# A one-core attention and gated-convolution kernel gets a new written order: first loads, zero fills and all later steps

## The chip, the cores and the metric

The kernel runs on one core of one Trainium2 chip. TensorE multiplies matrices, VectorE and ScalarE work on tiles, GpSimd takes a few two-operand rows and issues some transfers, and SyncE (SP) issues most transfers. The metric is device microseconds of one execution. Shown for the kernel before is the median of three runs; a profile is of one further execution.

## The reference

Inputs are `q`, `k`, `v` of 4 batches x 8 heads x 768 positions x 64, eight memory keys and values for each head, two 512x512 weights and a filter of 5 taps for each of 512 channels. Weights and filter come as 64-bit floats. Cut to what is computed:

```python
for c in range(S // 32):                      # chunks of 32 queries
    k_ctx = k[:, :, max(0, 32*c - 16) : min(S, 32*c + 40)]
    k_full = concatenate([mem_k, k_ctx]); v_full = ...same for v...
    scores = 0.125 * q_c @ k_full.T
    a = softmax(scores)
    out[chunk] = a @ v_full
x = out as (B, S, 512)
gate = sigmoid(sum over 5 taps of conv_w[t] * x shifted by t)     # causal
result = (gate * (x @ w_val)) @ w_out
```

## The kernel before

**Units.** Attention is cut into 20 units: one pair of heads and a span of positions (the first 256 positions of the first batch for units 0 to 3, its other 512 for units 4 to 7, and all 768 of one batch for units 8 to 19). For each unit `u` TensorE transposes K and Q (`tk`, `tq`) into PSUM, the steps `ek` and `eq` evict them, `sc` multiplies the scores, `mx` and `ss` on VectorE take maximum and shift, `ex` on ScalarE the exponential, `tp` transposes the probabilities, `ep` evicts them, `va` multiplies with V, `nd`, `ni`, `nx` divide by the sum, and `tx` transposes the result `x`. From `x` come a rounded part `xh`, its remainder `xl`, and the filter's sum in `gate`: the first tap `cv<u>_0_4` writes it, four more add to it on VectorE (L817, the last is `cv<u>_0`); `ga` is a tanh on ScalarE. `hs` and `hp` carry four columns over a span's edge.

**Pieces.** The two products with the weights run over eight pieces of positions (256, 512 and six of 384). `f1_n_co,ci` (L867) is three products of piece `n`: high with high, high with low, low with high. `h` multiplies by the gate, `hh` and `hl` split the result again, `f2` (L922) multiplies by the second weight, `oe` evicts, `st` stores.

**Weights.** Each of the eight 128-row blocks (`wv0` to `wv3`, `wo0` to `wo3`) is loaded raw (`lw0` to `lw7`, two buffers), and decoded in steps 1 to 8 on VectorE and ScalarE (step 1, L346, takes the exponent out, step 2, L352, the mantissa, step 7, L373, sets the sign, step 8, L379, is a product on VectorE or GpSimd); `h` and the bare name split it into a rounded part (a cast) and a remainder (L255). The filter goes the same way (`cw1` to `cw8`), is transposed by TensorE and copied.

**V tiles.** Three tiles in turn hold V in windows. Before the first three units they are filled with zeros and a column of ones (`zv0` to `zv2`, L276); loads `lv` put the windows in, and from unit 3 on `mv` copies the memory values in first. `mk` copies the memory keys, which TensorE has transposed once (`tmem`, evicted by `emem`), into the K tiles.

**What sets the order.** The string `ORDER` (lines 71 to 171) is the program's order, written out: each word names an engine (T TensorE, V VectorE, A ScalarE, G GpSimd, S SP) and a step, and each engine takes its own steps in that order. `Plan.run` issues them; waits between engines follow from the data and the buffers in `CAPS` (one buffer each for `x`, for the scores and values, for the transposes; three PSUM banks for the products). An engine that waits holds up everything behind it in its own queue, its transfers too.

## Time and profile before

| | us |
|---|---|
| median of three runs (268.54 to 270.05) | 268.61 |
| the profiled execution: its own time | 270.8 |
| its span, first to last instruction | 268.8 |
| TensorE busy (share of the span) | 240.4 (89%) |
| TensorE weight loads | 202.8 (75%) |
| VectorE | 209.9 (78%) |
| ScalarE | 130.4 (49%) |
| GpSimd | 74.2 (28%) |
| moved by transfers | 34.97 MB, 130 GB/s on the mean |

The profiled execution is 2.2 us longer than the median. Matmuls overlap in their pipeline, so TensorE's busy time hides short waits; the busy time of its weight loads shows better how densely it is fed. A row of a timeline or chain begins with its start in us from the first instruction and its length in us; an arrow `<-` in brackets names what ended the idle time before it. A row of a group gives count, total busy us and mean ns. A name ending in q (SPq, ACTq) is that engine's queue issuing a transfer.

### The profile page before, as it was taken

How to read it: one execution, taken by the hardware profiler on the slowest of the kernel's cores; microseconds unless marked ns; L12 is line 12 of the kernel's file. 1: busy time of each engine (PE TensorE's matmuls, PEld its weight loads, DVE VectorE, ACT ScalarE, POOL GpSimd, SP SyncE). 2: the span in 40 equal slices, each digit the busy share in tenths (PEclk: the TensorE clock that was granted, in tenths of full speed). 3: DMA queues.
4: the chain of work that ended last, by engine and by line, in shares of the span. 5: the costliest groups of instructions: out<-in, count | busy, mean ns of one | idle time of the engine just before them, and what ended most of it. 6: DMA issues, size and time to landing. Idle time of an engine off the chain costs nothing.

```text
span 268.8 us, 10223 instructions
## 1 busy us (share of the span) xinstructions
PE 240.4 (89%) x4478; PEld 202.8 (75%) x4478; DVE 209.9 (78%) x376; ACT 130.4 (49%) x240; POOL 74.2 (28%) x98
## 2 busy tenths in 40 slices
...
GB/s 155 173 167 196 202 181 197 184 208 158 140 197 178 156 151 156 195 109 206 114 160 124 58 147 160 184 182 179 25 82 80 2 2 80 79 0 41 39 78 78
DMA packets 88657, 34.97 MB, mean 130 GB/s; under 512 B 83794, under 2 KB 85350, under 8 KB 88614
## 3 DMA queue, kind: packets, MB, share of 16 engines
...
q10 hardware_dynamic: 320, 0.33, 0.5%
q14 instruction: 8, 0.07, 0.1%
HBM read 28.03 MB, written 6.29 MB: 128 GB/s over the span
## 4 chain that ended last, share of the span: by engine, by line
PE 51%; DVE 23%; DMA 8%; ACT 7%; issue 7%; SPq 1%; POOL 1%; POOLq 0%; ACTq 0%; DVEq 0%
PE vp L867 18%; PE op L922 12%; DVE gate L817 9%; PE sp L658 5%; PE xps L709 4%; PE tpx L769 4%; DMA v<-in_v_dram 4%; PE tp L588 3%; DMA mk_nat<-in_mem_k_dram 3%; DVE xl L255 2%; DMA kn<-in_k_dram 2%; PE tk L588 2%; PE tk L582 2%; ACT gate L821 2%; DVE xn L732 2%
## 5 line engine op out<-in xcount | busy, mean ns | idle before, releaser
L817 DVE SCALAR_TENSOR_TENSOR gate<-tpx,cw,gate 128x764 f32<-128x764 f32 (+4 forms) x80 | 67.7, 846 | 4.6 <-ACT gate L821 3.9
L867 PE MATMUL vp<-xh,wv_hi 128*128 128x384 f32 (+2 forms) x128 | 48.1, 376 | 0.1
L867 PE MATMUL vp<-xl,wv_hi 128*128 128x384 f32 (+2 forms) x128 | 44.1, 345 | 1.5 <-DVE xl L255 1.5
L867 PE MATMUL vp<-xh,wv_lo 128*128 128x384 f32 (+2 forms) x128 | 43.5, 340 | 0.0
L922 PE MATMUL op<-wo_hi,hh 128*128 128x512 f32 (+1 forms) x100 | 41.4, 414 | 0.0
L255 POOL TENSOR_TENSOR hl<-h,hh 128x384 fp32r<-128x384 f32 (+2 forms) x23 | 23.3, 1017 | 63.8 <-ACT hh L237 48.1
L922 PE MATMUL op<-wo_hi,hl 128*128 128x512 f32 (+1 forms) x100 | 38.5, 385 | 0.0
L922 PE MATMUL op<-wo_lo,hh 128*128 128x512 f32 (+1 forms) x100 | 38.5, 385 | 0.0
L963 POOL DMA_DIRECT2D out_dram<-o x22 | 12.1, 550 | 68.6 <-ACT o L952 43.7
L867 PEld LDWEIGHTS vp<-xl,wv_hi 128*128 128x128 f32 x128 | 24.3, 190 | 3.6 <-DVE xl L255 2.8
L867 PEld LDWEIGHTS vp<-xh,wv_hi 128*128 128x128 f32 x128 | 24.4, 190 | 2.3 <-ACT xh L237 0.3
L867 PEld LDWEIGHTS vp<-xh,wv_lo 128*128 128x128 f32 x128 | 24.5, 191 | 1.1 <-issue 0.2
L873 DVE SCALAR_TENSOR_TENSOR h<-gate,vp 128x384 f32<-128x384 f32 (+2 forms) x32 | 17.4, 547 | 9.5 <-PE vp L867 9.3
L237 ACT CAST hh<-h 128x384 fp32r<-128x384 f32 (+2 forms) x25 | 12.6, 508 | 21.7 <-DVE h L873 21.4
L658 PEld LDWEIGHTS sp<-kT,qT 64*32 64x32 f32 x1536 | 16.5, 107 | 8.0 <-issue 3.1
L658 PE MATMUL sp<-kT,qT 64*32 64x64 f32 x1536 | 20.0, 228 | 2.6 <-issue 0.9
L841 ACT ACTIVATE gate<-gate 128x768 f32<-128x768 f32 (+2 forms) x20 | 14.3, 716 | 16.5 <-DVE gate L817 13.5
L237 ACT COPY pT<-tp 128x384 f32<-128x384 f32 (+2 forms) x29 | 13.9, 478 | 16.5 <-PE tp L588 16.5
L922 PEld LDWEIGHTS op<-wo_hi,hl 128*128 128x128 f32 x100 | 18.8, 188 | 4.0
L709 PE MATMUL xps<-v,pT 64*32 64x65 f32 x1536 | 20.2, 229 | 0.9 <-DMA v<-in_v_dram 0.4
L709 PEld LDWEIGHTS xps<-v,pT 64*32 64x32 f32 x1536 | 16.8, 107 | 5.1 <-issue 2.2
L922 PEld LDWEIGHTS op<-wo_hi,hh 128*128 128x128 f32 x100 | 18.8, 188 | 2.3
(101 smaller groups left out, 436.3 us busy)
## 6 DMA issues: line engine op xcount, KB each, us to landing
out_dram<-o POOLq DMA_DIRECT2D x20, 256.0 KB, 3.0
...
```

The source lines that it names most:

```text
L237: return lambda: nc.scalar.copy(out(), in_())
L255: return lambda: eng.tensor_tensor(out=out(), in0=a(), in1=b(), op=ALU.subtract)
L588: nc.tensor.transpose(U[name, i][:, (g - g0) * P : (g - g0 + 1) * P], src(g), ident)
L658: nc.tensor.matmul(U["sp"][CH * jc : CH * (jc + 1), j, g * WIN : (g + 1) * WIN], U["qT"][j * D : (j + 1) * D, g * P + CH * jc : g * P + CH ...
L709: nc.tensor.matmul(U["xps"][CH * jc : CH * (jc + 1), j, g * VW : (g + 1) * VW], U["pT"][j * D : (j + 1) * D, g * P + CH * jc : g * P + CH ...
L769: nc.tensor.transpose(U["x", i][:, o : o + P], U["xn"][:, g].rearrange("p j d -> p (j d)"), ident,)
L817: nc.vector.scalar_tensor_tensor(out=o, in0=i_, scalar=w, in1=o, op0=ALU.mult, op1=ALU.add)
L841: nc.scalar.activation(g, g, AF.Tanh, scale=0.5)
L867: nc.tensor.matmul(vp, w, x, start=ci == 0 and m == 0, stop=ci == NCT - 1 and m == 2)
L873: nc.vector.scalar_tensor_tensor(out=T["h", n, co][:, 0:nt], in0=bt[b, co]["gate"][:, t0 : t0 + nt], scalar=1.0, in1=T["vp", n, co][:, 0:n ...
L922: nc.tensor.matmul(op, x, w[:, ci, c0:c1], start=ci == 0 and m == 0, stop=ci == NCT - 1 and m == 2)
L963: eng.dma_start(out[b, r0 : r0 + P, c0:c1], T["o", n, g, c0][:, 0 : c1 - c0])
```

## The change

Two edits. The zero fill of the V tiles shrinks: the whole tile is no longer filled; tile 0 gets zeros in its first window alone, and all three get their column of ones. And `ORDER` is another string, in nearly every line. Its 1141 steps are the same, but their places differ, and 96 of them run on another engine.

```diff
 ORDER = """
-V:bias0 G:ident S:lcw A:bias S:lk0 A:lq0 G:zv0 V:zv1 S:lq1 A:lk1 G:zk V:zm S:mem S:lv1_1 G:lw0
-V:cw1 A:cw4 V:cw2 G:lw1 V:cw3 S:lmv G:zv2 T:tk0_0 V:cw6 A:cw5 V:cw7 S:lv0_1 V:cw8 A:ek0_0 S:lv2_1
...
-G:st7_2 T:f2_7_02 T:f2_7_21_ T:f2_7_03 T:f2_7_22_ A:oe7_0 T:f2_7_23_ G:st7_0 A:oe7_2_ G:st7_2_
+V:bias0 G:ident G:lw0 S:mem S:lcw S:lk0 A:lq0 G:zv0 S:lv0_0 S:lv0_1 A:lk1 S:lq1 S:lw1 V:zv1
+S:lv1_0 S:lv1_1 V:zv2 S:lv2_0 S:lv2_1 V:zm A:bias G:zk V:cw1 G:lmv A:cw4 V:cw2 V:cw3 V:cw6 T:tk0_0
+A:cw5 V:cw7 G:cw8 A:ek0_0 S:lk2 T:tcw A:cw T:tk1_0 V:wv01 A:wv04 V:wv02 V:wv03 A:ek1_0 V:wv06
...
+A:oe7_0 T:f2_7_10 S:st7_0 T:f2_7_21_ T:f2_7_11 T:f2_7_22_ T:f2_7_12 T:f2_7_23_ T:f2_7_13 A:oe7_2_
+G:st7_2_ A:oe7_1 G:st7_1
 """
...
     for i in range(NV):
-        def zero_v(eng, t=v_tiles[i]):
-            eng.memset(t, 0.0)
+        def zero_v(eng, t=v_tiles[i], i=i):
+
+            if i == 0:
+                eng.memset(t[:, 0, 0:D], 0.0)
             eng.memset(t[:, :, D : D + 1], 1.0)
```

Three places show what the new string does on an engine. The first is VectorE from its fill of the memory values on, at the first weight; `craw`, `e_cw` and `m_cw` are the filter, `tp_mem` and `memT` the memory keys, `raw_wv0` the first weight. Before:

```order
L296 MEMSET mv_78 128x1024
L346 TENSOR_SCALAR e_cw_132<-craw_86 20x128
L352 TENSOR_SCALAR m_cw_133<-craw_86 20x128
L357 SCALAR_TENSOR_TENSOR m_cw_133<-craw_86,m_cw_133 20x128
L368 TENSOR_SCALAR e_cw_132<-e_cw_132 20x128
L373 SCALAR_TENSOR_TENSOR e_cw_132<-craw_86,e_cw_132 20x128
L379 TENSOR_TENSOR m_cw_133<-m_cw_133,e_cw_132 20x128
L240 COPY cw_77<-tp_cw_168 128x20
L240 COPY memT_75<-tp_mem_171 64x64 x2
L240 COPY kT3_71<-memT_75 128x24x8
L346 TENSOR_SCALAR e_wv0_196<-raw_wv0_130 128x512
```

The same place of VectorE now:

```order
L298 MEMSET mv_78 128x1024
L348 TENSOR_SCALAR e_cw_150<-craw_86 20x128
L354 TENSOR_SCALAR m_cw_151<-craw_86 20x128
L359 SCALAR_TENSOR_TENSOR m_cw_151<-craw_86,m_cw_151 20x128
L370 TENSOR_SCALAR e_cw_150<-e_cw_150 20x128
L375 SCALAR_TENSOR_TENSOR e_cw_150<-craw_86,e_cw_150 20x128
L348 TENSOR_SCALAR e_wv0_195<-raw_wv0_99 128x512
```

The filter's product and copy have gone to GpSimd and ScalarE, and the copies of the memory keys stand after the second weight now.

The second place is TensorE's start; `kn` and `qn` are raw K and Q, `sp0` the scores of unit 0. Before:

```order
L582 MATMUL tk0_0_144<-ident_67,kn0_101 64x64 x12
L439 MATMUL tp_cw_168<-ident_67,m_cw_133 128x20
L315 MATMUL tp_mem_171<-ident_67,mk_nat_76 128x128
L582 MATMUL tq0_0_182<-ident_67,qn0_104 64x64 x8
L658 MATMUL sp0_203<-kT0_68,qT0_199 32x64 x16
```

The same place of TensorE now:

```order
L584 MATMUL tk0_0_159<-ident_67,kn0_103 64x64 x12
L441 MATMUL tp_cw_179<-ident_67,m_cw_151 128x20
L584 MATMUL tk1_0_182<-ident_67,kn1_118 64x64 x12
L584 MATMUL tq1_0_203<-ident_67,qn1_121 64x64 x8
L584 MATMUL tq0_0_224<-ident_67,qn0_106 64x64 x8
L317 MATMUL tp_mem_250<-ident_67,mk_nat_76 128x128
L584 MATMUL tk2_0_259<-ident_67,kn2_176 64x64 x12
L660 MATMUL sp0_277<-kT0_68,qT0_247 32x64 x16
```

The first scores stand behind the transposes of units 1 and 2 as well.

The third place is VectorE at the end of piece 3; `h3_3` is that piece's last block, `ss14` the shift of unit 14's scores. Before:

```order
L679 TENSOR_REDUCE mx14_2659<-sp14_2585 128x12
L240 CAST xh20_2671<-tpx12_0_2469 128x768
L683 TENSOR_TENSOR ss14_2681<-sp14_2585,mx14_2659 128x2x6x64
L255 TENSOR_TENSOR xl20_2690<-tpx12_0_2469,xh20_2671 128x768
L240 COPY kT3_71<-tk15_1_2683 128x12x2x16
L873 SCALAR_TENSOR_TENSOR h3_2_2743<-gate12_2115,vp3_2_2562 128x384
L240 CAST hh3_2_2749<-h3_2_2743 128x384
L725 TENSOR_SCALAR den13_2755<-xps13_2693 128x12
L240 COPY pT14_2759<-tp14_0_2745 128x384
L728 RECIPROCAL den13_2755<-den13_2755 128x12
L732 TENSOR_TENSOR xn13_2766<-xps13_2693,den13_2755 128x2x6x64
L873 SCALAR_TENSOR_TENSOR h3_3_2781<-gate13_2315,vp3_3_2651 128x384
```

The same place of VectorE now:

```order
L875 SCALAR_TENSOR_TENSOR h3_1_2684<-gate11_1768,vp3_1_2636 128x384
L819 SCALAR_TENSOR_TENSOR gate20_2646<-tpx12_0_2617,cw_77,gate20_2646 128x767
L240 CAST hh3_1_2699<-h3_1_2684 128x384
L240 CAST xh20_2705<-tpx12_0_2617 128x768
L255 TENSOR_TENSOR xl20_2763<-tpx12_0_2617,xh20_2705 128x768
L677 MEMSET sp14_2714 32x2x16
L679 MEMSET sp14_2714 32x2x8
L681 TENSOR_REDUCE mx14_2771<-sp14_2714 128x12
L825 TENSOR_SCALAR gate21_2788<-tpx13_0_2774,cw_77 128x768
L255 TENSOR_TENSOR xl21_2797<-tpx13_0_2774,xh21_2786 128x768
L875 SCALAR_TENSOR_TENSOR h3_3_2806<-gate13_2310,vp3_3_2668 128x384
```

The shift of unit 14 and one eviction of its probabilities now come after this block, and the first tap and remainder of unit 13 before it.

More of the change, by code (lines that the diff above doesn't have):

```diff
@@ new lines @@
+V:wo27 A:cv1_0_4 V:ni2 S:lv5_1 V:mk8 A:ep4_0 V:nx2 V:cv1_0_0 A:wo25 T:va3 V:wo16 A:xh1_0 T:tq5_0
+S:lv5_0 V:cv1_0_1 G:wo28 A:mv6 V:nd3 V:xl1_0 V:cv1_0_2 T:f1_0_11 A:eq5_0 V:ni3 S:lq7 V:cv1_0
+T:f1_0_31 A:wo2h V:wo17 T:f1_0_01 A:ga1 S:lv6_0 T:tx2_0 G:wo2 T:tk8_0 V:wo18 A:xh2_0 A:hs2 A:ek8_0
+S:lw7 A:cv2_0_4 T:tq6_0 S:lk9 V:xl2_0 A:wo1h V:nx3 T:f1_0_32 S:lk10 V:cv2_0_0 A:eq6_0 G:wo1
+T:f1_0_12 V:cv2_0_1 T:va4 S:lq8 V:cv2_0_2 T:tq7_0 S:lv6_1 V:cv2_0 A:mv7 V:nd4 V:ni4 T:tx3_0
+T:f1_0_02 A:ga2 S:lv7_1 V:nx4 A:xh3_0 A:cv3_0_4 V:xl3_0 T:sc5 V:cv3_0_0 S:lv7_0 V:hs3 V:cv3_0_1
@@ new lines @@
+A:ga4 S:lv8_0 V:mx6 G:mk10 T:tx5_0 A:eq8_0 T:f2_0_03 V:hp5 V:ss6 A:cv5_0_4 T:tk10_0 V:xh5_0
+T:f2_0_12 A:ex6 V:oe0_0 A:ek10_0 T:va7 V:xl5_0 S:st0_0 T:tp6_0 V:cv5_0_0 G:mv10 T:f2_0_13 V:nd7
+V:ep6_0 T:f1_1_00 A:oe0_1 V:ni7 V:cv5_0_1 T:tq9_0 T:f1_1_10 V:nx7 G:st0_1 A:eq9_0 S:lv10_0
+T:f1_1_30 V:cv5_0_2 T:va6 V:cv5_0 S:lv10_1 T:tk11_0 A:ga5 V:nd6 G:mv9 T:tx7_0 V:ni6 A:ek11_0
+T:f1_1_31 A:xh7_0 V:hp7 V:nx6 T:tq9_1 A:cv7_0_4 V:xl7_0 T:f1_1_11 A:eq9_1 V:cv7_0_0 T:f1_1_01
+S:lv9_1 T:sc9 V:cv7_0_1 S:lv9_0 V:cv7_0_2 T:tk11_1 V:mx9 G:mk13 A:ek11_1 T:tq8_1 V:cv7_0 A:eq8_1
@@ new lines @@
+A:ep11_1 T:f1_2_00 T:tq13_0 T:tx10_0 A:eq13_0 T:va11 S:lv13_0 A:xh10_0 A:cv10_0_4 V:xl10_0
+T:tq12_0 S:lv13_1 G:mv14 T:f1_2_01 A:eq12_0 V:nd11 T:f2_1_31 V:cv10_0_0 T:tq12_1 V:ni11 T:f1_2_02
+V:cv10_0_1 A:eq12_1 T:f2_1_32 S:lv14_0 V:nx11 T:tq13_1 T:f1_3_00 A:eq13_1 V:cv10_0_2 S:lq14
+T:f2_1_33 T:sc12 S:lq15 V:cv10_0 A:oe1_3 S:st1_3 T:tk13_1 A:ga10 S:lv14_1 V:mx12 G:mk16 T:tx11_0
+A:ek13_1 T:f1_2_20 A:xh11_0 V:ss12 T:tk13_0 T:f1_3_01 A:cv11_0_4 S:lk14 V:xl11_0 T:f1_2_21 A:ex12
+T:f1_3_02 S:lk15 V:cv11_0_0 T:f1_2_22 A:ek13_0 T:f1_2_03 V:cv11_0_1 T:tp12_0 T:sc13 A:ep12_0
@@ new lines @@
+A:ek14_1 V:cv12_0_0 T:f2_2_11 S:lv16_0 T:tk15_1 V:cv12_0_1 T:f1_3_12 T:f1_3_30 V:ek15_1 T:f1_3_13
+V:cv12_0_2 T:tq15_0 T:f1_3_31 V:h3_1 A:eq15_0 T:f2_2_12 V:cv12_0 T:tk14_0 T:f1_3_32 V:hh3_1
+A:ek14_0 S:lk17 V:xh12_0 T:f2_2_00 G:hl3_1 A:ga12 T:sc14 V:xl12_0 T:tq17_0 V:mx14 G:mk18 T:tx13_0
+A:eq17_0 T:f2_2_01 A:xh13_0 V:cv13_0_4 T:tk15_0 T:f1_3_33 V:xl13_0 A:ek15_0 S:lk16 T:f2_2_02
+V:h3_3 T:tq15_1 T:f2_2_13 V:cv13_0_0 A:eq15_1 S:lq16 T:f2_2_03 V:ss14 A:oe2_1 T:tq17_1 G:st2_1
+T:f2_3_10 A:oe2_0 V:cv13_0_1 S:lq18 A:ex14 T:sc15 S:st2_0 V:cv13_0_2 A:eq17_1 T:tp14_0 A:mk19
@@ new lines @@
+T:f2_3_21 A:ga14 S:lv18_0 T:tx15_0 A:ek17_1 V:ss16 T:f2_3_22 A:cv15_0_4 T:tk17_0 V:xh15_0
+T:f1_4_11 A:ex16 S:lk18 T:f2_3_23 V:cv15_0_0 A:ek17_0 S:lk19 T:f1_4_00 A:oe3_2 V:xl15_0 T:sc17
+G:st3_2 V:cv15_0_1 T:tp16_0 V:mx17 T:f1_4_01 A:ep16_0 T:f1_4_30 T:tp16_1 V:cv15_0_2 T:f1_4_02
+A:ep16_1 T:f1_4_31 V:ss17 T:tq19_0 T:f1_4_12 V:cv15_0 A:ex17 T:va16 A:eq19_0 A:ga15 T:tp17_0
+V:nd16 T:f1_4_13 V:mv19 A:ep17_0 T:f1_4_03 V:h4_1 T:tp17_1 S:lv19_1 T:f1_4_32 V:ni16 A:ep17_1
+V:h4_0 T:f1_4_20 A:hh4_1 V:nx16 T:tq18_0 A:hh4_0 S:lv19_0 G:hl4_1 T:f1_5_00 A:eq18_0 T:f1_4_21
```

160 lines of the change are left out of this document (64 added, 96 removed).

## The prediction

> **What bounds the kernel now.** I read the busy time by stage first, then the chain that ended last, and then the first 30 us instruction by instruction. By stage (length, then busy us and instruction count of TensorE, its weight loads, VectorE, ScalarE and GpSimd, the granted clock, the DMA share, GB/s):
>
> ```profile
> 0.00:30.20 30.20, 16.25 (x286) 13.06 (x286) 22.99 (x50) 12.90 (x27) 11.77 (x29) 1.00 0.62 168
> 30.20:60.00 29.80, 23.82 (x664) 19.47 (x664) 28.02 (x64) 21.53 (x48) 13.11 (x12) 1.00 0.96 200
> 75.50:130.00 54.50, 51.95 (x1157) 41.71 (x1155) 47.44 (x80) 29.88 (x50) 10.48 (x12) 1.00 1.03 166
> 130.00:239.00 109.00, 108.58 (x1963) 94.82 (x1962) 90.89 (x144) 48.45 (x82) 23.41 (x28) 1.00 0.56 100
> 239.00:268.80 29.80, 24.75 (x132) 22.09 (x130) 5.54 (x10) 5.13 (x10) 7.88 (x11) 0.95 0.14 53
> ```
>
> VectorE is busy 94% of 30 to 60 us, where it splits the weights beside attention. From 75 to 130 us neither it (87%) nor the weight loads (77%) are full; from 130 us TensorE has no idle time (weight loads 87%). In the middle stage the chain of waits runs through VectorE's filter taps:
>
> ```profile
> 97.72 1.02 DVE gate L823
> 99.60 0.92 DVE gate L817
> ...
> 127.90 0.97 DVE xl L255
> 128.91 0.98 PE vp L867 x4
> ```
>
> So up to 129 us a gain must come from VectorE's queue, and behind it from TensorE's. At the start one load holds everything, as the chain of the first 40 us shows:
>
> ```profile
> 3.77 6.81 DMA mk_nat<-in_mem_k_dram
> ...
> 10.71 0.46 PE tp_mem L315
> ...
> 11.44 0.23 DVE memT L240
> ```
>
> The two copies of the memory keys stand in VectorE's queue ahead of the first weight, so that row begins at 12.36 us, although its load, issued at 3.11, was there by 9.6 (both rows below).
>
> **The change part by part.** *The head start.* These rows of the first 30 us carry it (start, us, engine, line):
>
> ```profile
> 0.74 1.28 ACT L265 ACT_TABLE_LOAD   x1 [0.74 <-PEq L984]
> 1.20 1.36 DVE L276 MEMSET v<- 128x1560 f32 x1 [0.29 <-issue]
> 2.16 2.97 ACTq L506 DMA_DIRECT2D kn<-in_k_dram  x2
> 3.11 1.22 POOL L402 DMA_DIRECT2D raw_wv<-in_moe_w_val_dram  x2
> 5.85 0.40 ACT L362 ACTIVATE e_cw<-e_cw,bias_e 20x128 f32<-20x128 uint32 x1 [3.62 <-DVE e_cw L346]
> 7.87 3.02 SPq L506 DMA_DIRECT2D v<-in_v_dram  x2
> 12.36 0.56 DVE L346 TENSOR_SCALAR e_wv<-raw_wv 128x512 uint32<-128x512 uint32 x1
> 13.06 0.77 SPq L506 DMA_DIRECT2D v<-in_v_dram  x2
> 13.92 0.68 PE L658 MATMUL sp<-kT,qT 64*32 64x64 f32 x32 [0.55 <-ACT qT L237]
> 15.98 0.42 DVE L346 TENSOR_SCALAR e_wv<-raw_wv 128x512 uint32<-128x512 uint32 x1
> 17.52 1.24 SPq L506 DMA_DIRECT2D kn<-in_k_dram  x2
> 20.65 0.69 DVE L373 SCALAR_TENSOR_TENSOR e_wv<-raw_wv,e_wv 128x512 uint32<-128x512 uint32 x1
> 21.50 1.54 PE L582 MATMUL tk<-ident,kn 64*64 64x64 f32 x24
> ```
>
> And the weight's loads, from issue to landing:
>
> ```profile
> DMA to landing us min/median/max: 4.1/4.9/6.5
> ```
>
> The first weight's load moves ahead of GpSimd's fills: issued near 1.3 us in place of 3.11, it lands between 5.4 and 7.8. The memory-key copies leave the place ahead of it on VectorE, and the fill of 1.36 us goes too. What is late next is ScalarE: its four load issues, which end at 5.13 us, now stand ahead of its table load, which ran beside them. 4.9 plus 1.28, 0.2 for a constant and 0.40 for the exponent of the filter weights make 6.8; VectorE needs two short rows more (about 0.5). The first weight row then starts near 7.4 us, 5.0 earlier.
>
> Three things take this back. (a) The second weight's load moves from GpSimd to SP, behind six other loads at about 0.62 each (two K loads take 1.24) and seven V loads at 0.39 (two take 0.77): 0.74 + 3.7 + 2.7 = 7.1 us, so with 0.6 for its issue and 4.1 to 4.9 to land it is there near 12, not at about 8.5; its first row, now at 15.98, comes near 12. (b) On TensorE the first score product, which ran at 13.92, now stands behind the transposes of the third key block, and that block's load stands on SP behind twelve V loads: 7.7 + 12 x 0.39 + 1.24 = 13.6, and 4.1 to land (the best of the weights; none of a K block is shown) gives 17.7. The transposes take 1.54 and the product 0.68, so it ends at 19.9. (c) VectorE has finished the second weight, a query copy, four small copies and a cast by about 17 and waits 3 us for that product, with all later weights and maxima queued behind the wait. With 0.5 for the maximum it stands at 20.4 us with two weights and the first maximum done; before, it had these and a subtraction of 0.42 at 20.65 + 0.69 = 21.34. The 5.0 us are spent: I take 0 for the whole start, with the ends -5.0 (nothing late behind the first weight) and +6.7 (first rival).
>
> *VectorE's work up to the last first-layer product of piece 3* (152.7 us before). I count the steps that stand ahead of that point in one table and not in the other, or have changed engine. Prices:
>
> ```profile
> L683 DVE TENSOR_TENSOR ss<-sp,mx 128x768 f32<-128x768 f32 x12 | 11.4, 952 | 0.2
> L953 DVE TENSOR_SCALAR o<-op 128x512 f32<-128x512 f32 x8 | 5.5, 684 | 3.9 <-PE op L922 3.9
> L823 DVE TENSOR_SCALAR gate<-tpx,cw 128x768 f32<-128x768 f32 x4 | 4.1, 1016 | 3.2 <-ACT xh L237 3.2
> L255 DVE TENSOR_TENSOR hl<-h,hh 128x384 fp32r<-128x384 f32 x6 | 3.3, 552 | 1.2 <-ACT hh L237 1.2
> L240 DVE CAST hh<-h 128x384 fp32r<-128x384 f32 x6 | 2.8, 464 | 0.1
> L240 DVE COPY qT<-tq 128x384 f32<-128x384 f32 x4 | 2.2, 549 | 0.1
> L379 DVE TENSOR_TENSOR m_wv<-m_wv,e_wv 128x512 f32<-128x512 f32 x2 | 1.8, 911 | 0.1
> ```
>
> Out go the fill 1.36, a weight's product and remainder 0.9 + 0.7, three first taps 2.8 (one on 512 columns), two output copies 1.4, four evictions 2.2, three casts 1.3, two remainders 1.2, one score shift 0.95 and small ones 1.6: 14.4 us. In come seven evictions 3.8, four casts 1.8, one weight's product and another's cast 1.3, a tap 1.0, two remainders 1.0, an output copy 0.7, a cast of 512 columns 0.7 and small ones 1.9: 12.2. VectorE reaches the point with 2.2 us less behind it.
>
> *TensorE at the same point.* Its prices, from the chain between 160 and 200 us:
>
> ```profile
> 162.88 0.66 PE tpx L769 x6
> 163.53 0.70 PE op L922 x3
> 164.24 0.33 PE tq L588 x3
> ```
>
> Ahead of the point now stand two more second-layer steps (1.4), three more key or query transposes (1.0) and one more x transpose (0.66), and two probability transposes fewer (0.66): 2.4 us more is done. If VectorE alone paces the time to there, the point comes 2.2 earlier with 2.4 less left: -4.6. If TensorE alone does, its lead is only work done sooner at the same rate: 0. I take the VectorE end, since the chain runs through its taps from 97 to 129 us, and keep both. ScalarE and GpSimd, which receive the moved rows, have room: 29.88 and 10.48 busy of 54.50.
>
> *The end.* The last output tile is now 512 columns wide, not 256, and its eviction and store follow the last product:
>
> ```profile
> L952 ACT ACTIVATE o<-op 128x512 f32<-128x512 f32 x15 | 9.0, 597 | 17.7 <-PE op L922 17.5
> out_dram<-o POOLq DMA_DIRECT2D x20, 256.0 KB, 3.0
> out_dram<-o POOLq DMA_DIRECT2D x2, 128.0 KB, 2.2
> ```
>
> The store lands 0.8 later; the eviction ends 0.4 later, of which 0.3 was a wait behind another store's issue before. That is +0.9.
>
> Sum: 0 - 4.6 + 0.9 = -3.7 us. The profiled execution took 270.8 us, 2.0 more than its span of 268.8, and 2.2 above the median of the three runs; I apply the difference to the median: 268.61 - 3.7 = **264.9 us**. About 1% (2.7 us) is what a measurement here tells from no change, so faster means under 265.9 and slower over 271.3.
>
> **The rivals.** *First, slower: SP's queue becomes the start's bound.* The row at 7.87 shows two V loads that took 3.02 us to issue, while the weights moved, against 0.77 later. If half of the twelve V loads behind the second weight go at that price, the third key block is late by 6 x 1.12 = 6.7 us, the first score product with it, and VectorE's queue behind that: 264.9 + 6.7 = 271.6. It decides from the point where that product ends after 19.9 + 3.7 = 23.6 us. For it speaks that row; against it, that GpSimd now has half a megabyte in flight then, not a whole one. [...] Chance 0.17.
>
> *Second, no change: TensorE paces already.* Its 108.58 busy of 109 speak for it: then nothing is won by 152 us, the waits before 130 us come back elsewhere, and 0 + 0.9 gives 269.5. Against it stands the weight loads' 77% in the middle stage. Chance 0.20.
>
> *Third, slower: GpSimd's added subtractions hold up VectorE.* The mantissa rows of the value weights spread like this:
>
> ```profile
> L352 DVE TENSOR_SCALAR m_wv<-raw_wv x4: 564/1114/1825, 12.8 to 30.1; 128x512 uint32<-128x512 uint32 x4
> ```
>
> The one of 1.82 us ran beside a GpSimd product. The new table gives GpSimd six two-operand rows more (five remainders, net, and one of the weights); at 1.82 - 0.56 = 1.26 each this adds 7.6: 272.5. Against it: most VectorE rows read PSUM, and the taps of the chain above keep to 0.92 to 1.02 us. [...] Chance 0.07.
>
> *Fourth, faster still: the head start is kept*, because the K block lands in 2 us and TensorE has the scores early: up to 4.4 of the 5.0, 260.5. Chance 0.11.
>
> **How the numbers follow.** The forecast has 0.45, of which 0.36 lies under 265.9 and 0.09 within 1%. Faster: 0.36 + 0.11 = 0.47. Same: 0.09 + 0.20 = 0.29. Slower: 0.17 + 0.07 = 0.24. The range runs from the fourth rival's 260.5 to the first one's 271.6.
>
> **What would show it.** In the new profile the first weight row should start near 7.4 us and the first score product end near 20, with VectorE idle some 3 us ahead of it; the second weight's first row near 12. The last first-layer product of piece 3 should end about 2 us earlier than 152.7, with weight loads over 77% of the stage before it. The last store should be issued a microsecond after the last product. A first score product after 24 us would make me wrong at the start; a middle stage with VectorE idle more than the 7 us of now, in the middle term.

## The result, and the profile after

The changed kernel takes **278.05 us** (median of four runs, 277.52 to 283.29) against 269.33 for the kernel before beside it: 1.030 times as long, 95% interval 1.0242 to 1.0359. The same kernel timed once more gave 279.79 us, 1.0272 (1.018 to 1.0364). I had forecast 264.9, with 271.6 as the upper end; it is 13 us slower than the forecast and 8.7 slower than before. The profiled execution took 283.29 us (span 281.5), 5.2 over its median; medians here count every execution, the ratios leave out disturbed ones like this, and its rows below are read together with later profiles of the same order.

The stages of after, cut as those of before were (length, then busy us and count of TensorE, its weight loads, VectorE, ScalarE, GpSimd, the granted clock, the DMA share, GB/s):

```profile
0.00:30.20 30.20, 13.95 (x246) 10.89 (x246) 16.35 (x43) 11.92 (x26) 9.26 (x25) 1.00 0.73 178
30.20:60.00 29.80, 23.86 (x518) 19.80 (x522) 22.33 (x57) 18.97 (x40) 12.02 (x10) 0.89 0.63 156
75.50:130.00 54.50, 51.94 (x1178) 42.20 (x1179) 45.57 (x80) 31.14 (x54) 16.83 (x19) 0.97 0.87 140
130.00:239.00 109.00, 107.11 (x2047) 92.53 (x2046) 91.28 (x141) 49.51 (x86) 23.41 (x29) 1.00 0.61 111
239.00:281.50 42.50, 36.94 (x197) 33.08 (x195) 14.45 (x21) 10.14 (x17) 11.89 (x15) 1.00 0.15 56
```

The records of TensorE's products overlap, so a row of them is shorter than its products added up: before, the first 64 score products are 0.31 us each at the median, and the row of the first 32 is 0.68. What has changed most is the first 60 us. By then VectorE has worked 38.7 us, where it had worked 51.0; in 30 to 60 us it was busy 94% and is busy 75% now. In two later profiles of this order it has worked 43.9 us (the same kernel again) and 41.7 (with more buffers, below) by then, so part of the 12.3 belongs to this one execution. The stages from 75 us on look much as before. The last first-layer product of piece 3, the point that the prediction reckoned with, stands in TensorE's timeline of after here:

```profile
166.67 0.34 PE L869 MATMUL vp<-xl,wv_hi 128*128 128x384 f32 x1
```

And of before here:

```profile
152.31 0.34 PE L867 MATMUL vp<-xl,wv_hi 128*128 128x384 f32 x1
```

It ends 14.4 us later. From it to the end of the span there were 116.1 us (268.8 - 152.65) and are 114.5 (281.5 - 167.01). So the whole loss of this profile lies ahead of that product and 1.7 us of it come back behind; the 12.7 us between the spans are 14.4 - 1.7. In four other profiles of the new order or of small changes to it (below) the product ends between 162.2 and 164.7, 9.5 to 12 us late, and TensorE has 109.3 us to go from there to its last product in all of them, where before it had 111.1 (263.75 - 152.65).

What VectorE waits for in the first 74 us tells the two kernels apart (total us, number of times, longest). Before:

```profile
DVE memT L240 <- ACT memT L237: 3.9, 2, 3.6
DVE sp L675 <- PE sp L658: 0.8, 1, 0.8
DVE bias_e L259 <- PEq L984: 0.8, 1, 0.8
DVE den L725 <- PE xps L709: 0.6, 1, 0.6
```

After:

```profile
DVE sp L677 <- PE sp L660: 4.9, 2, 3.4
DVE e_wv L348 <- DMA raw_wv<-in_moe_w_val_dram: 3.7, 3, 1.9
DVE e_wv L370 <- ACT e_wv L364: 3.1, 1, 3.1
DVE xl L255 <- ACT gate L823: 2.0, 1, 2.0
DVE den L727 <- PE xps L711: 2.0, 1, 2.0
DVE sp L679 <- PE sp L660: 1.7, 2, 1.2
DVE e_wo L370 <- ACT e_wo L364: 1.3, 1, 1.3
```

One long wait for the memory keys has been traded for a dozen waits for all three neighbours: TensorE's scores, ScalarE's exponents, weights still on their way. Up to the last first-layer product of piece 3, VectorE's work and idle time read so, before, after, and in the order of after with more buffers (columns as in the table of stages above):

```profile
0.00:152.65 152.65, 129.73 (x2883) 106.58 (x2884) 133.34 (x256) 89.48 (x170) 51.80 (x68) 1.00 0.91 163
0.00:167.01 167.01, 138.83 (x2898) 115.82 (x2899) 129.33 (x258) 89.22 (x168) 50.89 (x67) 0.96 0.82 153
0.00:164.41 164.41, 137.83 (x2898) 114.44 (x2899) 130.42 (x258) 89.42 (x168) 51.73 (x67) 0.97 0.83 158
```

VectorE does somewhat less work by then and stands idle 19.3 us before (152.65 - 133.34), 37.7 after, 34.0 with more buffers. To compare kernels that do the steps in different orders earlier on, I count each VectorE step at one fixed price, its usual duration, and ask when 80 us of such work are done and how long VectorE has stood idle by then. Before: at 92.4 us, 10.5 idle. After: at 101.7 us, 26.7 idle. The 9.3 us of delay are 16.2 more of waiting, less 6.9 because the steps themselves ran nearer to their usual price; with the small fills alone they already ran 3.6 nearer. Which prices are called usual moves these figures by one or two us, and in other profiles of the new order (again, more buffers, with fillers) the waiting is 10 to 12 us more than before, not 16.

### The profile page after: what moved, and what is told of

Read it like the earlier page. It is cut to its first block, busy times and chain, and to the rows that moved or that the text cites. A ratio compares the mean times of both kernels' runs of the same rounds, so it can differ in the third digit from the quotient of the medians.

```text
span 281.5 us, 10215 instructions
## 1 busy us (share of the span) xinstructions
PE 247.1 (88%) x4478; PEld 209.5 (74%) x4478; DVE 202.1 (72%) x368; ACT 131.8 (47%) x242; POOL 76.7 (27%) x99
## 4 chain that ended last, share of the span: by engine, by line
PE 56%; DVE 17%; DMA 8%; issue 7%; ACT 6%; SPq 3%; POOL 1%; ACTq 1%; POOLq 0%; DVEq 0%
PE vp L869 17%; PE op L924 15%; DVE gate L819 8%; PE xps L711 5%; PE sp L660 4%; DMA kn<-in_k_dram 4%; PE tpx L771 4%; PE tp L590 3%; DMA v<-in_v_dram 3%; SPq L508 3%; DVE xl L255 2%; PE tk L584 2%; DMA raw_wv<-in_moe_w_val_dram 2%; PE tq L584 2%; PE tk L590 2%
## 5 line engine op out<-in xcount | busy, mean ns | idle before, releaser
L255 POOL TENSOR_TENSOR hl<-h,hh 128x384 fp32r<-128x384 f32 (+2 forms) x28 | 28.2, 1012 | 72.3 <-ACT hh L237 58.9
L869 PE MATMUL vp<-xh,wv_lo 128*128 128x384 f32 (+2 forms) x128 | 43.9, 343 | 0.0
L869 PEld LDWEIGHTS vp<-xh,wv_lo 128*128 128x128 f32 x128 | 25.1, 196 | 1.2
L869 PEld LDWEIGHTS vp<-xl,wv_hi 128*128 128x128 f32 x128 | 24.9, 195 | 0.8
L237 ACT COPY qT<-tq 128x384 f32<-128x384 f32 (+2 forms) x28 | 13.5, 480 | 24.1 <-PE tq L590 17.0
L660 PE MATMUL sp<-kT,qT 64*32 64x64 f32 x1536 | 21.4, 237 | 3.2 <-issue 2.5
L965 POOL DMA_DIRECT2D out_dram<-o x19 | 10.5, 555 | 50.1 <-ACT o L954 35.6
L660 PEld LDWEIGHTS sp<-kT,qT 64*32 64x32 f32 x1536 | 17.4, 112 | 8.9 <-issue 6.3
L237 ACT COPY kT<-tk 128x384 f32<-128x384 f32 x29 | 13.7, 473 | 20.8 <-PE tk L584 12.2
L584 PE MATMUL tk<-ident,kn 64*64 64x64 f32 x192 | 12.2, 304 | 12.7 <-DMA kn<-in_k_dram 10.8
L255 DVE TENSOR_TENSOR xl<-tpx,xh 128x768 fp32r<-128x768 f32 (+2 forms) x20 | 15.9, 793 | 10.0 <-ACT gate L823 9.7
```

The lines of the kernel that those rows point to most:

```text
L237: return lambda: nc.scalar.copy(out(), in_())
L255: return lambda: eng.tensor_tensor(out=out(), in0=a(), in1=b(), op=ALU.subtract)
L584: nc.tensor.matmul(to[rows_, n_], flat[rows_, n_ * D : (n_ + 1) * D], ident[rows_, rows_], start=True, stop=True,)
L660: nc.tensor.matmul(U["sp"][CH * jc : CH * (jc + 1), j, g * WIN : (g + 1) * WIN], U["qT"][j * D : (j + 1) * D, g * P + CH * jc : g * P + CH ...
L869: nc.tensor.matmul(vp, w, x, start=ci == 0 and m == 0, stop=ci == NCT - 1 and m == 2)
L965: eng.dma_start(out[b, r0 : r0 + P, c0:c1], T["o", n, g, c0][:, 0 : c1 - c0])
```

## The experiments

Ratios are to the kernel before, run beside each on the same chip, with 95% intervals. The rivals for the cause were: the first loads (SP's queue), TensorE running at half rate, buffers that hold the transfers up, a stall of TensorE while instructions are loaded, and, my own first theory, the in-order rows' waits for one another in the new order of the computing steps.

### Which part of the change costs

Four kernels take the change apart. The first keeps the old order and takes the small zero fills alone, the lower half of the diff of the change; all later kernels have these small fills too.

> The order of before, word for word, with the small zero fills alone. Before is 269.3 us, after 278.0. Both theories of the loss (the first loads; the new order of the first 40 us) say that the fills are no part of it. VectorE's 1.36 us fill lay ahead of 3.6 us in which VectorE had nothing to do, so both expect 268.5 to 270. If the fills were the cause (more DMA writes meeting less memory time, a wait that was hidden), it would be 275 or more.

The second adds the new first loads, up to that of the third key block, and keeps everything else in the old order:

```diff
-V:bias0 G:ident S:lcw A:bias S:lk0 A:lq0 G:zv0 V:zv1 S:lq1 A:lk1 G:zk V:zm S:mem S:lv1_1 G:lw0 V:cw1
-A:cw4 V:cw2 G:lw1 V:cw3 S:lmv G:zv2 T:tk0_0 V:cw6 A:cw5 V:cw7 S:lv0_1 V:cw8 A:ek0_0 S:lv2_1 T:tcw V:cw
+S:mem S:lcw S:lk0 V:bias0 G:ident A:lq0 A:lk1 A:bias G:lw0 G:zv0 S:lv0_0 S:lv0_1 S:lq1 S:lw1 V:zv1
+S:lv1_0 S:lv1_1 G:zk V:zm V:cw1 A:cw4 V:cw2 V:cw3 G:lmv G:zv2 S:lv2_0 S:lv2_1 T:tk0_0 S:lk2 V:cw6 A:cw5
...
```

> The small fills, and the first loads of after (all of them up to the load of the fourth unit's keys: order, queue and engine), with every other step in the order of before. Theory 1 (the loads: the V loads and the second weight load stand ahead of the third unit's keys on SyncE's queue, and the attention chain starts late for that) expects most of the loss here, 275 to 279 us. Theory 2 (the loss is made by the order of the computing steps: decoding ahead of the attention chain, three score products ahead of the first value product) expects 266 to 270, since the first score product needs only the first two loads and stands first again.

The third begins in the old order and goes on in the new one; the fourth does the opposite. In both the steps of the first part stand as in their own order, and all that is left follows in the other's.

```diff
-ORDER = (new order)
+ORDER = (old order up to A:hh0_0, near 54 us) + (what is left, in the new order)
```

> The steps of before through the first gated tile of piece 0 (the cast after h0_0, 54 us of before), then all other steps in the order of after, small fills. Theories 1 and 2 (the loss is made in the first 41 to 66 us) expect 266 to 270 us. Theory 3 (the rest of the new order, 54 us to the end, loses by itself) expects 275 or more. By the traces 12 of the 14 us at the last product of piece 3 were late by the first product of piece 0 already, so if the rest costs 2 us it would be 271.

```diff
-ORDER = (new order)
+ORDER = (new order up to A:xh4_0, near 70 us) + (what is left, in the old order)
```

> The other half: the steps of after through the fifth unit's normalised tile (about 80 us of after), then all other steps in the order of before, small fills. Theories 1 and 2 expect it as slow as after, 275 to 280 us. Theory 3 expects 268 to 271.

| kernel | median us | ratio |
|---|---|---|
| small fills, old order | 269.51 | 0.9925 (0.9883 to 0.9966) |
| small fills, new first loads, old order | 269.70 | 0.9943 (0.9897 to 0.9989) |
| old front, new rest | 278.03 | 1.0241 (1.016 to 1.0321) |
| new front, old rest | 281.19 | 1.0369 (1.0282 to 1.0455) |

The fills and the first loads are worth a little over half a per cent together, on the good side; by themselves they are cleared. (The new order with the old first loads was not run, so what the loads do inside the new order is not shown; a kernel with the old loads, the third of the table, loses 2.4% without them.) With the new loads and the old order VectorE's waits of the first 74 us are one for the filter's transpose and small change:

```profile
DVE cw L234 <- PE tp_cw L435: 4.0, 1, 4.0
DVE e_cw L342 <- DMA craw<-in_moe_conv_w_dram: 1.2, 1, 1.2
DVE e_cw L364 <- ACT e_cw L358: 1.1, 1, 1.1
DVE memT L234 <- ACT memT L231: 1.1, 2, 0.8
```

It has 80 us of work done at 89.8 us, 2.6 earlier than before. The loss lies in the order of the computing steps, with the engine that each runs on, and both halves of that order carry it: each half alone costs about as much as the whole. The parts do not add, which already speaks against a single wait. All of these kernels have the small fills: against the old order with them (0.9925) each of the losses here and below is 0.8% larger.

### Where in the order

Three more seams, and the changed kernel again beside them:

```diff
-ORDER = (new order)
+ORDER = (new order up to T:sc0, near 23 us) + (what is left, in the old order)
```

> The steps of after through its 79th line of the order (first loads, first two weight rows, the third unit's key transposes, the first score product, which ends at 22.8 us there against 14.6 us before), then all other steps in the order of before, small fills. Theory L (the late first score product alone makes the loss; rival 1 of the prediction) expects most of the loss: 275 to 279 us. Theory D (it is made by what follows: three score products ahead of the first value product, and each queue standing behind that) expects 269 to 272.

```diff
-ORDER = (new order)
+ORDER = (new order up to S:lk5, near 32 us) + (what is left, in the old order)
```

> The same with 42 more steps of after, through the softmax of the third score product, the first value product behind it, and the load of the sixth unit's keys ahead of the fourth unit's values on SyncE's queue. Theory D expects 274 to 278 us here, 4 or more above the run that stops at the first score product. Theory L expects the same time in both. If both come out within 1% of 269.5, the loss is made after 31 us only.

```diff
-ORDER = (new order)
+ORDER = (old order up to V:cv10_0_1, 112 to 122 us) + (what is left, in the new order)
```

> The steps of before through 112 us (589 of 1141), then the order of after, small fills. The run that changes over at 54 us gave 278.0. By the time at which TensorE has done the same work, that run lost its 6 to 8 us between 55 and 85 us of before and nothing later, and after loses nothing past about 85 us. So 268 to 272 is expected here by both theories; 275 or more would say that the last two thirds of the new order lose by themselves.

> The kernel after unchanged, beside the other runs of this call, for a profile without the extra 5 us of the first one: 277 to 279 us.

Measured: 276.53 us, 1.0157 (1.0066 to 1.0248); 273.97, 1.0144 (1.005 to 1.0238); 274.12, 1.0128 (1.0045 to 1.0211); and 1.0272 for the changed kernel. The 23 us up to the first score product cost some 1.5% by themselves, whether one goes on in the old order at once or after the third score product. That is what theory L had foretold for the pair, the same time in both, and both forecasts of theory D missed: no 269 to 272 for the first, and no 4 us more for the second. So a front that brings the first score product late costs about half of the loss. It isn't all of it: with the old front, whose first score product starts at 13.74 us, the new rest still costs 2.4%. The part behind 112 us costs 1.3% on top of the old front, where 268 to 272 us had been forecast; in the changed kernel nothing is lost there any more. So a seam has a price of its own too, and the table can't be read as a sum; what it does speak against is a cause that sits in one stretch.

### TensorE at half rate

Around 42 us of after, instructions of one form change their duration. Of TensorE's timeline (start, us), a group of key transposes, and two equal first-layer products, one on each side of the change:

```profile
39.61 1.54 PE L584 MATMUL tk<-ident,kn 64*64 64x64 f32 x24
...
41.68 0.41 PE L869 MATMUL vp<-xl,wv_hi 128*128 128x256 f32 x1
...
43.93 0.28 PE L869 MATMUL vp<-xl,wv_hi 128*128 128x256 f32 x1
```

And before, at 30 us:

```profile
30.30 0.92 PE L582 MATMUL tk<-ident,kn 64*64 64x64 f32 x24
```

The same 24 products take 1.54 or 0.92 us, the same single product 0.41 or 0.28. By these durations, and by the granted clock from 42 us on, TensorE's work at half rate lies in 3.7 to 30.3 us before (16.4 us of it) and in 6.6 to 42.2, 49.1 to 55.9, 66.0 to 69.5 and 93.5 to 96.9 us after (36.3 us). The column of the granted clock shows 1.00 up to 30 us in both, so it does not show the first of these stretches. Half of the 20 us more at half rate would be 10 us, an estimate, and as much as the loss. In the later three stretches, 6.8, 3.5 and 3.4 us long, the column reads 0.50, 0.53 and 0.50, and first-layer products equal to those above take 0.41 us again (at 55.08 and 67.39 us). Whether this is the cause is another question, and that TensorE comes off half rate sooner when it has less idle time was my guess. To test both I put products of the identity with itself, which nobody reads, into TensorE's waits of the first 38 us: 91 of them in the new order (12 places; the expectation below says 87), 59 in the old one, 51 in the old one with the new loads (8 places each; the expectation says 65); the trace has two records for each.

```diff
+    WARM = [20, 3, 2, 4, 4, 6, 20, 4, 16, 4, 4, 4]
+    def warm(i, n):
+        T["warm", i] = buf([P, 512], "f", f"warm{i}", pool=ps)
...
+            nc.tensor.matmul(T["warm", i][:, 0:P], ident, ident, start=True, stop=True)
-S:lv1_0 S:lv1_1 V:zv2 S:lv2_0 S:lv2_1 V:zm A:bias G:zk V:cw1 G:lmv A:cw4 V:cw2 V:cw3 V:cw6 T:tk0_0
+S:lv1_1 V:zv2 S:lv2_0 S:lv2_1 V:zm A:bias G:zk V:cw1 G:lmv A:cw4 V:cw2 V:cw3 V:cw6 T:warm0 T:tk0_0 A:cw5
```

> The order of after, with 87 matmuls of 128 x 128 that nobody reads put into TensorE's waits of the first 38 us (20 ahead of the first key transposes, 20 ahead of the third unit's, 16 ahead of the first value product, 2 to 6 at nine other places). Theory C (the clock): by the durations of its own instructions TensorE ran at half rate to 42.2 us of after, and again from 49.1 to 55.9, 66.0 to 69.5 and 93.5 to 96.9, with 36.3 us of its busy time in those stretches, against 16.4 us up to 30.3 in before; half of the difference is 10 of the 12.5 us at the last product. With TensorE kept busy the first 42 us run at full rate: half of 23.4 us of busy time, less what only turns into waiting, 4 to 9 us, so 269 to 274. Theory W (the waits): the half rate only goes with waits that the order makes, TensorE is waited for by nobody there, and the fillers change nothing or cost their length: 277 to 281.

> The order of before with the small fills, and 59 such matmuls in TensorE's waits of the first 26 us (8 ahead of the first key transposes, 16 ahead of the memory's transpose, 14 ahead of the first transposed score tile, 3 to 6 at five places). The same without fillers is 269.5 us, with half rate up to 24.4 us in the profiled run and 11.3 us of busy time in it. Theory C: up to half of that, 2 to 5 us, so 264 to 268. Theory W: 269 to 271.

> The order of before with the first loads of after and the small fills (269.7 us; half rate up to 23.6 us, 10.6 us of busy time in it), and 65 such matmuls in TensorE's waits of the first 26 us (20 ahead of the first key transposes, 14 ahead of the first transposed score tile, 2 to 4 at six places). Theory C: 265 to 268 us, the best of all. Theory W: 269 to 271.

The fillers did what they were put in for. Of TensorE's timeline in the filled new order:

```profile
1.36 6.16 PE L266 MATMUL warm<-ident 128*128 128x128 f32 x40 [1.36 <-POOL ident masks.py:199]
...
7.45 0.92 PE L593 MATMUL tk<-ident,kn 64*64 64x64 f32 x24
...
21.79 0.98 PE L593 MATMUL tk<-ident,kn 64*64 64x64 f32 x24
```

Half rate is left from 1.4 to 4.4 us (the first 40 of these records take 6.16 us, 40 later ones, from 17.23, take 4.63) and behind 274 only, and the kernel takes 278.12 us, 1.0283 (1.0232 to 1.0333): what it took without them. In the old order the fillers cost 1.9% (272.39, 1.0113, 1.0034 to 1.0193, against 0.9925 for the same kernel without them), with the new loads about 0.6% (270.31, 1.0007, against 0.9943). If they cost the same in the new order, full rate has given back 0.6 to 1.9%, some 2 to 5 us of the 8.7; what they do cost there is not shown. (They are not free where they stand: the third key block's transposes begin at 21.79 us behind them, 20.59 without.) What the trace does show is that the waits are there at full rate too: in the filled new order the last first-layer product of piece 3 still ends at 162.16 us, 9.5 late, and VectorE has stood idle 31.2 us by then (162.16 - 130.98), against 34.0 with more buffers and no fillers and 19.3 before. For the most part the half rate isn't what makes the waits.

I also tried the opposite cure, attention of the first units ahead of the later key transposes, so that TensorE's first products follow each other as early as the data allow:

```diff
-T:tk2_0 A:mk3 V:mk0 V:mk1 A:mk2 V:wv1h T:sc0 G:wv1 A:ek2_0 S:lk4 T:tk3_0 V:mx0 V:wv21 V:ss0 A:wv24
...
+V:eq0_0 V:wv17 T:tmem A:emem11 A:emem00 V:emem10 G:wv18 S:lw3 V:emem01 A:mk3 V:mk0 T:sc0 V:mk1 A:mk2
+V:wv1h G:wv1 V:mx0 V:wv21 V:ss0 T:sc1 A:ex0 T:tp0_0 A:wv24 V:wv22 V:mx1 A:ep0_0 V:wv23 V:ss1 T:va0
+T:tk2_0 S:lk4 V:wv26 A:ex1 V:nd0 A:ek2_0 V:ni0 A:wv25 T:tq2_0 V:nx0 A:eq2_0 T:tp1_0 A:ep1_0 T:tx0_0
...
```

> The order of after, its first loads and its zero fills, with only the attention chain of the first two units moved forward on TensorE, VectorE and ScalarE: the first two score products ahead of the third unit's key transposes, both value products, the first unit's transposed tile and the first first-layer product ahead of the third score product. Theory W and theory C both expect a gain, since the waits of 4.0 us (keys) and 2.5 us (third score's softmax) no longer stand ahead of the first first-layer product, which comes some 8 to 12 us earlier and with it full rate: 268 to 273. If the loss is made later than 42 us, by the steps that are left in the new order, it stays at 276 or more.

Both theories missed. It is the slowest of all: 284.62 us, 1.0534 (1.0474 to 1.0595). Its first score product begins at 19.15 us (22.15 in after), but its chain of waits (start, us) then hangs on the first output weight, whose load begins at 34.46 and holds VectorE until 38.7:

```profile
34.11 0.34 DVE mx L676
34.46 4.25 DMA raw_wo<-in_moe_w_out_dram
38.73 0.43 DVE e_wo L343
```

### Buffers

The chain of after in the first 40 us runs through transfers:

```profile
15.73 4.72 DMA kn<-in_k_dram
...
20.59 1.63 PE tk L584 x23
22.22 0.69 PE sp L660 x32
...
23.29 5.40 DMA raw_wv<-in_moe_w_val_dram
```

The first is the third key block, the last the fourth weight. These two don't wait for a buffer: the raw key buffers were free from 8.9 and 11.6 us, when the transposes of units 0 and 1 had ended, the raw weight buffer from 17.5, when the second weight's step 7 had. They stand in SP's queue behind other loads, and SP there also waits for earlier loads to land, longest for one of memory values, from the first half of the third key block (15.73) to its second (17.89):

```profile
SPq L508 <- DMA v<-in_mem_v_dram: 1.7, 1, 1.7
```

A buffer does hold SP from 28.2 to 33.5 us, until the transposes of unit 4's keys give up a raw key buffer. One buffer more for keys and for weights:

```diff
-    a=1, t=1, x=1, f=3, kn=2, qn=2, qT=2, ss=2, pT=2, xn=1, xh=4, xl=4, gate=5, h=2, hh=7, hl=7,
-    o=3, ew=2, mw=2, wraw=2,
+    a=1, t=1, x=1, f=3, kn=3, qn=2, qT=2, ss=2, pT=2, xn=1, xh=4, xl=4, gate=5, h=2, hh=7, hl=7,
+    o=3, ew=2, mw=2, wraw=3,
```

> The order of after with three buffers instead of two for raw keys and for raw weights, so that the load of the sixth unit's keys need not wait at 28 us for the fifth unit's transposes (SyncE's queue stood there for 5.2 us, and the DMA engines were 17% busy from 30 to 35 us). Theory Q (SyncE's queue standing at a buffer makes the loss) expects 270 to 274. Theory D expects 276 to 279, since the computing steps stand in the same rows.

278.50 us, 1.0256 (1.0172 to 1.034): no change. That stand of SP is gone, and the key load that stood until 33.46 is issued at 27.99:

```profile
26.18 1.77 SPq L399 DMA_DIRECT2D raw_wo<-in_moe_w_out_dram  x1
27.99 1.10 SPq L503 DMA_DIRECT2D kn<-in_k_dram  x2
```

VectorE still waits 5.2 us for scores and 3.3 for one exponent of ScalarE in the first 74 us. These two buffers are cleared; SP now stands 4.6 us until 48.0 for ScalarE's copy into one of the three V tiles, whose number was left as it was.

### Moving the waits away by calculation

If waits between in-order rows are the cause, then moving a step that waits behind one that could run should win. I replayed the orders with the durations of the traces, moved single steps within their engines' rows as long as the replay said that the end came earlier, and ran the outcome: 247 steps of the new order, 310 of the old, about as many of the old with the new loads.

```diff
-V:bias0 G:ident G:lw0 S:mem S:lcw S:lk0 A:lq0 G:zv0 S:lv0_0 S:lv0_1 A:lk1 S:lq1 S:lw1 V:zv1
...
+V:zv1 G:lw0 S:lk0 S:lcw V:zm S:lw1 A:lq0 A:lk1 V:bias0 A:bias G:ident V:cw1 G:zk G:zv0 V:cw2 A:cw4 V:zv2
...
```

> The order of after, its loads, fills and engine for every step, with 247 of the 1141 steps moved within their engine's row, in the first 200 places of TensorE, VectorE and ScalarE (about 95 us) and in the rows of SyncE and GpSimd. The moves were chosen by replaying the order with the step durations and landing times of the traces, so that steps stand less ahead of what they wait for. Theory D (the loss is waits that in-order queues make in the first 95 us, whatever the loads, engines and clock) expects it all back: 266 to 271 us. If it is the engines of the 96 steps that changed over, the contention at one time, or the last two thirds of the order, it stays at 275 or more.

> The same treatment of the order of before with the small fills (269.5 us without it): 310 steps moved within their engine's row, none to another engine. Theory D expects 262 to 267 us. If before has no such waits left on its path, 268 to 271.

> The same treatment of the order of before with the first loads of after and the small fills (269.7 us without it). Theory D expects 262 to 267 us, within 1% of the run on before's own first loads.

They took 276.12 us, 1.0166 (1.0092 to 1.024); 274.81, 1.0102 (1.0015 to 1.019); and 278.08, 1.0241 (1.0162 to 1.032). The replay promised gains for all three. The new order won about a per cent; the old order lost 1.8% to its own unmoved form (1.0102 against 0.9925), and with the new loads 3% (1.0241 against 0.9943). Theory D missed all three, and the first by the mark set for it, 275 or more: beside the last two thirds of the order that leaves the engines of the 96 steps that changed over and the contention at one time, which no run takes apart. What the three runs do show is that fixed durations and the order of the rows don't give the time of this kernel.

### TensorE's stands for instructions

In 42 to 125 us of after, TensorE's longest waits have no releaser:

```profile
PE sp L660 <- issue: 2.5, 2, 1.8
```

Before there is one of 0.9. The largest stands in the middle of one unit's score product, after 27 of its 64:

```profile
62.66 0.44 PE L660 MATMUL sp<-kT,qT 64*32 64x64 f32 x27 [0.43 <-DVE xn L734]
64.89 0.63 PE L660 MATMUL sp<-kT,qT 64*32 64x64 f32 x37 [1.79 <-issue]
```

Its operands can't be what is missing half way through: the last copy into a K or Q tile ahead of it ended at 59.37 us. Counted over TensorE's records, every such stand inside a product lies 193 or 194 instructions past a multiple of 256. As this one begins, a packet of 16,384 bytes is under way on the queue that carries instructions (62.07 to 63.37 us); beside the stands under 1 us there is mostly none:

```profile
q8 instruction: 35, 0.57, 0.9%
```

35 packets of 16,384 bytes are the 0.57 MB, one for each 256 of TensorE's roughly 9,000 instructions (4,478 products and as many weight loads in the profile). At this place the 250 instructions before it had taken some 3.5 us (the expectation below counts 3.3), and TensorE stood 1.8, 2.5, 2.9 and 1.2 us in four profiles (after, after again, more buffers, new front); where the 250 had taken 4.0 to 5.0 it stood anything from 0 to 2.5, and stands of 1.1 and 1.6 came behind 250 that took 5.7 and 6.4 (both in the old order with the new loads, as it was and with steps moved). That the stands are instructions being loaded is argued from this period and these packets, not shown. To take the stand away I put slower instructions in between: a value product and two first-layer steps moved ahead of this score product in the new order, and in the old order one second-layer step ahead of a key transpose and a score product near 108 us.

```diff
-S:lw7 A:cv2_0_4 T:tq6_0 S:lk9 V:xl2_0 A:wo1h V:nx3 T:f1_0_32 S:lk10 V:cv2_0_0 A:eq6_0 G:wo1
-T:f1_0_12 V:cv2_0_1 T:va4 S:lq8 V:cv2_0_2 T:tq7_0 S:lv6_1 V:cv2_0 A:mv7 V:nd4 V:ni4 T:tx3_0
...
-T:f1_0_03 V:wo31 A:eq7_0 T:f1_0_33 V:mx5 A:mk9 T:f1_0_13 S:lq9 A:wo34 V:h0_0 V:wo32 T:f1_0_20
+A:ek8_0 S:lw7 A:cv2_0_4 T:tq6_0 S:lk9 V:xl2_0 A:wo1h V:nx3 T:va4 S:lk10 V:cv2_0_0 A:eq6_0 G:wo1
+T:f1_0_32 V:cv2_0_1 T:f1_0_12 S:lq8 V:cv2_0_2 T:tq7_0 S:lv6_1 V:cv2_0 A:mv7 V:nd4 V:ni4 T:tx3_0
...
+T:f1_0_33 V:wo31 T:sc5 A:eq7_0 V:mx5 A:mk9 T:f1_0_13 S:lq9 A:wo34 V:h0_0 V:wo32 T:f1_0_20 A:hh0_0 V:wo36
```

> The order of after, with one value product moved ahead of two first-layer steps, and two later first-layer steps put ahead of the second unit's score product behind it, all on TensorE's row near 55 to 65 us, so that the 250 instructions ahead of the stand at 61.9 us (2.5 us, without a releaser, then half rate from 61.9 to 68.4) take some 5.3 instead of 3.3 us. Nothing else is changed. Theory F (instruction loading: the stand and the half rate behind it are part of the loss) expects the stand gone and 273 to 276 us. If the stand only covers a wait that would come anyway, 277 to 280.

```diff
-V:ss10 T:f2_1_31 A:eq11_1 A:cv9_0_4 T:tk12_1 V:xl9_0 T:sc11 A:ex10 V:cv9_0_0 A:ek12_1 T:f2_1_32 V:mx11
+V:ss10 T:f2_1_31 A:eq11_1 A:cv9_0_4 T:f2_1_32 V:xl9_0 T:tk12_1 A:ex10 V:cv9_0_0 A:ek12_1 T:sc11 V:mx11
```

> The order of before with the small fills (269.5 us), with one second-layer step moved ahead of the twelfth unit's score product at 104 us, so that the 250 instructions ahead of the stand seen there (0.5 us in one profile, 2.2 to 2.5 us with 3.4 us of half rate behind it in two others) take 5.0 instead of 4.1 us. Theory F expects no stand there, and 267.5 to 269.5 us with less spread. Otherwise 269 to 271, by the delay of the score product.

In the new order it worked and was worth nothing: 278.83 us, 1.031 (1.0244 to 1.0375).

```profile
PE xps L706 <- issue: 1.7, 2, 1.2
...
PE sp L655 <- issue: 0.7, 2, 0.4
```

The stand in the scores is down to 0.3 (0.4 at another place), TensorE is at full rate from 42.7 to 274.8 us, and two waits without a releaser, of 1.2 and 0.5, now stand ahead of value products; they lie 212 and 180 instructions past a multiple of 256, so they are no stands of this kind. In the old order the move missed: a stand of 2.0 us still came at 108.5 us, and the kernel took 270.17, 0.9957 (0.9918 to 0.9996), as with the small fills alone. So the stands are real, but taking away a single one, with the half rate behind it, is worth nothing here; what all of them together cost was not found.

## Why the prediction was wrong

**The head start, forecast 0 with the ends -5.0 and +6.7: too small.** Its parts were seen. The first weight row starts at 6.11 us (forecast 7.4), the second weight's at 13.71 (12), the first score product runs from 22.15 and ends at 22.8 (19.9), and VectorE stands 3.40 us for it (3):

```profile
6.11 0.43 DVE L348 TENSOR_SCALAR e_wv<-raw_wv 128x512 uint32<-128x512 uint32 x1 [0.51 <-DMA raw_wv<-in_moe_w_val_dram]
10.65 0.43 DVE L370 TENSOR_SCALAR e_wv<-e_wv 128x512 uint32<-128x512 f32 x1 [3.05 <-ACT e_wv L364]
13.71 0.67 DVE L348 TENSOR_SCALAR e_wv<-raw_wv 128x512 uint32<-128x512 uint32 x1 [1.90 <-DMA raw_wv<-in_moe_w_val_dram]
22.96 0.09 DVE L677 MEMSET sp<- 32x32 f32 x1 [3.40 <-PE sp L660]
```

What I hadn't priced is the second of these rows. ScalarE's exponent of the first weight stands behind two evictions in ScalarE's row, which wait for TensorE, which waits for the first key load:

```profile
8.91 0.48 ACT L237 COPY kT<-tk 128x384 f32<-128x384 f32 x1 [3.57 <-PE tk L584]
...
9.90 0.72 ACT L364 ACTIVATE e_wv<-e_wv,bias_e 128x512 f32<-128x512 uint32 x1
```

VectorE's wait of 3.05 us there is in part made good, since its next stand, 1.90 us, is for the second weight's load. The product's 2.9 us come from the key load, issued from 15.73 and not complete until 20.45 instead of 17.7, its second half behind SP's wait of 1.7 us. VectorE has the first maximum at 23.51 (23.09 + 0.42), not at 20.4. Part of this is that one execution: in the other profiles of this front the product ends between 21.1 and 23.2 us. It is the first rival's mechanism (SP's queue ahead of the third key block), with its product 0.8 us short of the 23.6 from which it was to decide. The loads alone don't do it: in the old order the same loads cost nothing; the first score product stands ahead of the third key block's transposes there, and starts at 13.48 us. The new order up to this product, with the old order behind it, costs 1.57%, about 4.2 us, where I had put 0.

**VectorE's and TensorE's work up to piece 3's last first-layer product, forecast -4.6: this is the step that failed.** The product came 14.4 us later in the profile of after, 9.5 to 12 later in the others, not 2.2 earlier. The count of moved work was no great error: TensorE's way from the product to its last one is 1.8 us shorter (111.1 and 109.3), of the 2.4 that I had counted, and VectorE has done 129.3 us of work by the product instead of 133.3. The error was the sentence "if VectorE alone paces the time to there": from 94% busy between 30 and 60 us I took it that VectorE's queue would be worked off at the same density in any order. The density belonged to the old order. In the new one VectorE is idle 33 to 38 us up to the product instead of 19.3, most of the difference by the time it has done 80 us of work. A row taken in order waits whenever its next step's input is late, as VectorE's did for 3.05 and 3.40 us above, and I had compared what stands ahead of a point on each engine, never whether a neighbour would have each input ready. I had named the sign that would show it, "a middle stage with VectorE idle more than the 7 us of now"; it idles 8.9 there (54.50 - 45.57), and 7.5 in 30 to 60 us, where it had idled 1.8.

**The end, forecast +0.9: measured +0.1.** The last eviction and store follow the last product in the order worked out: last product's end at 276.34, eviction to 277.03, store issued at 277.32, 1 us after the product. But from the last product to the end of the span there are 5.1 us (281.5 - 276.34), and before there were 5.0 (268.8 - 263.75).

```profile
275.94 0.40 PE L924 MATMUL op<-wo_hi,hl 128*128 128x512 f32 x1
276.43 0.60 ACT L954 ACTIVATE o<-op 128x512 f32<-128x512 f32 x1 [0.36 <-PE op L924]
277.32 0.54 POOL L965 DMA_DIRECT2D out_dram<-o  x1 [0.42 <-ACT o L954]
```

**The rivals.** The second, no change because TensorE paces already, falls with the stage of 60 to 95 us, where TensorE was busy 33.38 us before and is busy 30.90 now (29.9 and 31.2 in two later profiles):

```profile
60.00:95.00 35.00, 30.90 (x675) 24.95 (x668) 28.98 (x65) 21.01 (x41) 8.98 (x10) 0.93 1.00 156
```

Before:

```profile
60.00:95.00 35.00, 33.38 (x707) 25.46 (x707) 32.08 (x65) 22.64 (x43) 10.48 (x11) 1.00 1.15 170
```

The third, GpSimd's rows holding up VectorE, goes the other way: VectorE's steps ran 6.9 us nearer to their usual price than before. The fourth, a head start that is kept, falls with the first score product at 22.8, and at 21.1 or later in every profile of this front. The slower side carried 0.24, and none of its prices reached the result; the third rival's 272.5 lay outside the range that I gave, 260.5 to 271.6, all the same.

**What stays open.** Shown: the fills and the first loads by themselves are not the cause, and the old order keeps its time with both; the new places and engines of the steps cost some 3%, and appear as waits of VectorE for its three neighbours; a third buffer for the raw keys and weights gives nothing back, nor does taking one stand of TensorE away; VectorE's waits remain when TensorE runs at full rate. Half rate may still make 2 to 5 of the 8.7 us, if the fillers cost in the new order what they cost in the old. The loss is spread over the front and the rest, each of which costs 1 to 4% alone. Not run: the new order with the old first loads, and the new places with the old engines of the 96 steps. Which of the moved steps start the waits was not isolated, and my replay with measured durations could not find them; that the remainder is the ripple of many small waits is argued from the totals, not shown.
